# Two quantities in one PSUM bank per half of the heads, the u row spread by one product, and a new written-out order

## The chip, the cores and the metric

The kernel runs on one core of one Trainium2 chip. The metric is the device time of one launch in microseconds (us). The core has a tensor engine for matrix products (PE, with its weight loads shown as PEld), a vector engine (DVE), a scalar engine (ACT), a third elementwise engine (POOL), and a queue that does nothing here but issue DMAs (SP). Each engine takes its instructions strictly in the order in which the program lists them; between engines semaphores hold an instruction back until what it reads is there. Inputs and outputs lie in device memory and are moved by 16 DMA engines.

## The reference

```python
B, H, S, D = 4, 8, 768, 48                       # r, k, v, w: [B, H, S, D]; u: [H, D]
state = zeros(B, H, D, D)
for t in range(S):
    cur   = einsum('bhd,bhe->bhde', u * k_t, v_t)
    y_t   = einsum('bhd,bhde->bhe', r_t, state + cur)
    state = w_t[..., None] * state + einsum('bhd,bhe->bhde', k_t, v_t)
x = y.transpose(0, 2, 1, 3).reshape(3072, 384)
h = x @ w_in                                     # [384, 2048]
out = maximum(0.01 * h, h) @ w_out               # [2048, 384], float32 out
```

It is a recurrent attention with a decay w per channel, whose output goes through two dense layers with a leaky rectifier between them. The kernel computes the attention in chunks of time steps. Within a chunk the decays are summed as logarithms, r is multiplied by exp of the sum and k by exp of minus the sum; products of the two (scores), masked to earlier steps and multiplied by v, give the part of y from inside the chunk, and the state carried from the chunk before gives the rest. The u term is added through the sum over d of u, k and r, times v.

## The kernel before, in words

The 3072 rows are 24 chunks of 128 steps (n = 0 to 23), six for each of the four sequences. The first four chunks are handled as two **pairs** by `pair` (n = 0 and n = 2): 256 steps of one sequence at a time, two neighbouring steps (j = 0, 1) on one partition, so 128 partitions hold 256 steps. The other chunks go through `single`, alone or two together (`run`). The dense layers run over 14 blocks of one or two chunks (`BLOCKS`): steps `up` (first layer: six products of 128x256 for a block of two chunks, or twelve of 128x128 for a block of one), `g` (the rectifier on ACT, PSUM to SBUF), `down` (second layer: four products of 128x384 per step, four steps per chunk), `ocopy` (PSUM to SBUF) and `store` (a DMA on SP).

A pair runs through these steps: `ln` of w (ACT); `cum`, products with fixed triangular matrices that sum the logarithms (PE); `total`, the sum over a chunk, and `adep`, its exp; four exps (ACT, in PSUM); four `rk` products of exp with r or k (DVE, the tiles `rk`); PE transposes of `rk` into PSUM, copied to the tile `rkT` by ACT or DVE; `scores` (PE), masks (DVE, tile `m`), then `intra`, `inter` and the u term's `addvs` (PE), a copy to `y`, transposes of y and copies into `xT`, the input of `up`. Beside it POOL makes `ru` (u times k, times r) and `vs`, DVE sums it (`dg`), and POOL casts v to bf16 (`vb`). Pair 0 does this in two halves of the heads (`PARTS`), each of its exps, `rk` products and copies being half as wide (128x192); pair 2 does it with all heads at once (128x384). In each case one PSUM bank holds one of four quantities: exp for k at j = 0 and 1, exp for r at j = 0 and 1.

The row u (384 numbers) is loaded by a DMA on ACT's queue, split by DVE into bf16 parts, and spread over 128 partitions by three PE products with one row each (`u_spread`), then copied to `ub`. Before that the PE multiplies zeros (`zero`).

A single chunk has `ln`, `cum`, `ci`, two exps (`er`, `ek`), two `rk`, transposes by PE or, for the chunks of `RK_DMA`, by a DMA transpose on SP (rkT<-rk), `scores`, two masks, `sums` and `state`, `intra`, `yadd`, and transposes of y by PE or, for `Y_DMA`, by DMA (xT<-y).

The order of all steps, and the engine of each, is not made at run time: `TABLE` lists them in one sequence (P is PE, V DVE, A ACT, G POOL, S SP, Z a product of zeros), `HOMES` says which buffer of a pool each step's tile takes, and `Steps.issue` writes them out. A buffer that is to be reused makes the later step wait for its readers. Lines: `mult`'s tensor operations are L231, `copy`'s L237 (DVE) and L239 (ACT), all PE products but the transposes L242, transposes L353 and L384, the pair's loads L400, its `ln` L417, its exps L456, weights' loads L299, single chunks' loads L618, `g` L858, stores L830.

Of the kernel before, what the change touches and what calls it, by code (L numbers as in the profile page):

```python
# [8 lines left out]
BF16 = mybir.dt.bfloat16  # L9
AF = mybir.ActivationFunctionType  # L10
# [53 lines left out]
PARTS = {0: [(0, 2), (2, 4)]}  # L64
HALVES = 'wkr'
# [6 lines left out]
WIDE = {'rkT', 'm', 'y', 'rk'}  # L72
TABLE = """
A0 S11 P1066 S6 A1 S9 S7 S8 V2 S10 V3 S12 Z512 Z512 Z512 Z512 Z512 Z512 Z256 Z192 P4 S88 A13 Z128 P16 V5 P17 A27
P15 A26 S153 A14 A24 Z512 Z160 P18 V31 G58 A25 P19 V28 A40 P21 S89 A43 V37 G62 P32 A41 V44 P29 A22 V53 P1067 P38
A33 P45 V30 A23 P54 V34 A39 P20 G59 S90 V46 P35 V55 A42 V50 A36 V47 P51 G63 P70 V60 A52 P48 A92 V71 G61 S147 V64
P94 V72 G57 S145 P93 A102 P95 G65 V49 A99 P96 S91 P73 A101 G56 P81 A98 V75 A97 P76 A100 G154 P77 V74 P79 S151
V106 P66 S156 G121 P78 V103 P107 A82 V67 P104 G117 P83 V108 A105 P80 P68 V112 A84 V85 G155 P113 A69 V109 A114
P86 V148 A87 P110 G118 S149 A111 P740 S159 A146 G122 P129 V119 P132 V131 A741 P732 S162 G116 V134 P730 G120 A733
V123 P738 G115 A731 V130 G124 A152 P125 V133 P136 A739 V126 S165 P138 P135 S171 P137 P127 A158 V157 P736 S168  # L80
V139 A128 P742 S173 V142 A737 P140 V150 P744 A743 A141 P143 P734 A745 V144 P758 V161 G160 A735 P768 A759 P760
A769 P752 A761 V163 P746 A164 S252 P770 P762 A771 P766 V167 A763 G166 S201 P764 A175 A767 P177 P772 S172 A765
V178 P753 A179 S200 A773 P754 A180 V169 G170 P747 S231 V181 P748 A256 P183 S174 P749 V184 G216 P258 S202 V750
P755 A260 A261 V259 P774 G187 A756 S253 V182 A263 P775 A262 G188 P185 A204 S757 P780 V186 S229 V189 P206 P191
S203 V207 P776 V193 A208 G176 P777 S295 A209 V192 G190 P194 P781 A778 V211 G217 A195 V210 P196 P214 S254 P782
V197 A215 G270 V265 P198 P212 V218 S232 A199 P783 A213 P268 A233 P790 S230 V269 A784 P220 A791 G205 P235 S785
V222 P788 G219 A238 A237 S356 V236 P223 P786 A789 G297 S327 V221 G251 A224 P792 A787 V264 S292 G274 P225 A239
P266 A793 P794 V226 G234 A240 V241 P227 G271 P795 V267 S779 A228 V242 P243 S255 P804 G247 V272 A244 S324 P245
A805 P278 G248 P802 V246 S293 V279 P275 A803 G358 V249 P796 G329 V284 G250 P797 S294 V276 A296 P806 V285 A798
S353 P298 V277 A807 P800 G257 V299 S799 P280 G273 A801 P286 S326 P288 V281 A303 P808 S376 V287 A328 A302 V289  # L90
P282 P330 G310 A300 P809 V305 S355 A283 A332 V331 A301 P290 P308 G311 A291 P810 V304 A335 V309 S436 P822 G314
A334 V312 A333 P306 A357 P824 G313 S325 A823 P359 A307 G343 V336 P318 P826 S378 A362 V319 A361 A825 G375 P315
V360 A380 P811 S354 V317 A364 P382 A827 V316 P828 S377 A385 A812 V383 P820 A829 G449 P320 S419 A386 P814 A821
V321 G339 A363 P816 V337 S416 A815 V365 P347 A387 G340 P322 V388 P818 S338 A817 V348 A384 P390 A819 P367 G398
V366 P830 A368 V391 S437 G371 V341 P402 P369 P831 V389 S473 A370 G342 V403 P392 P832 V323 A393 G372 P846 S751
A420 P399 G421 V373 A847 S435 G394 P422 V408 S418 P842 A425 A424 V401 G434 P344 A843 P833 S813 V423 G374 S417
V346 P848 A427 A834 G450 V400 P844 A849 S492 V409 P404 A426 G395 P850 A845 V451 S835 V405 P836 S471 V396 A439
P406 V345 P837 A407 S491 V428 P441 P349 A443 P838 V442 S633 V350 A444 P851 A445 G453 V429 A446 P351 V447 P839
G430 S438 V352 P458 V448 P858 A840 V459 G431 S454 P862 A859 P860 A475 V432 A863 P477 G433 P856 A861 V478 S841
G504 P864 A479 S490 A857 P866 A482 G646 A865 P872 A867 G505 P870 A480 A481 S545 P873 G440 A871 V506 S379 G489  # L100
P874 V483 P466 G452 P455 S524 V467 P852 V457 S472 P853 V465 P868 A494 V464 S543 A854 P496 V456 A869 P468 P878
V497 S474 V469 A499 P460 A501 G381 P879 S470 A500 V461 G397 A498 P410 V503 P412 A528 V411 P462 P880 S544 A463
V413 G508 P530 V484 S581 P414 P875 A533 V502 G485 A415 S493 V531 P881 A876 G486 A535 P888 V882 S877 A532 A534
P884 G476 S509 V487 A889 G542 P898 A885 P513 A547 G488 P916 V514 A899 P549 G557 A917 S883 P890 V550 S526 P894
G558 A552 A553 P912 A891 V555 G495 A895 V559 P896 G507 A551 A554 P519 S525 P886 A913 G561 V556 S598 A897 P892
V520 A887 P510 S546 A893 P900 V512 P920 S599 V517 P914 V518 S601 P901 V536 A915 V511 G538 P521 S579 P902 V537
G539 V522 A602 P515 S562 P903 V516 G560 P604 V540 A904 P918 V605 G548 P906 A607 G612 A919 S523 P574 A608 P907
V575 A609 G603 P908 A606 V611 G616 P909 A583 P627 P585 V910 P921 S905 A588 V628 A587 S580 G597 P922 V586 S600
# [881 lines left out]
```

## Time and profile before

| | us |
|---|---|
| median of 3 runs | 182.56 (180.97 to 182.56) |
| the profiled execution | 181.88 |
| its span in the profile | 180.1 |
| PE busy in the span | 171.3 |
| ACT busy | 118.6 |
| DVE busy | 112.2 |
| POOL busy | 101.3 |

A span runs from the first to the last instruction; the time of an execution holds 1.8 us more. A row of the timeline gives start, duration, engine, line, operation, what it writes and reads, and how many instructions were merged; in brackets, how long the engine had been idle and what ended that. A row of a group gives the total busy time and the mean of one instruction in ns. A busy PE is not a PE at its peak, since its products overlap; how long one takes in a stream is read from the start of a row and the start of the next.

### The profile page before, as it was taken

The page shows a single profiled execution, that of the slowest core. Times are in us where ns is not written, and L with a number is a line of the kernel's source. Part 1 is how long each engine was busy: PE and PEld are TensorE (multiplying, and loading weights), DVE is VectorE, ACT ScalarE, POOL GpSimd, SP SyncE. Part 2 cuts the span into 40 slices and gives each one's busy share as a digit, 9 for nine tenths or more (in the row PEclk, how much of TensorE's full clock was granted, in tenths as well). Part 3 has the DMA queues.
Part 4 walks back from the last instruction along what each step waited for, and adds up shares of the span by engine and source line. Part 5 has one row for each costly group of instructions (what it writes and reads, how often), then busy time and mean ns, then how long its engine had stood idle before and what let it go on. Part 6 is the DMA issues. An engine that isn't in the chain of part 4 may idle for free.

```text
span 180.1 us, 5012 instructions
## 1 busy us (share of the span) xinstructions
PE 171.3 (95%) x1960; PEld 128.1 (71%) x1960; DVE 112.2 (62%) x230; ACT 118.6 (66%) x265; POOL 101.3 (56%) x137
## 2 busy tenths in 40 slices
PE   7978899999999999999999999989999999999992
PEld 2645688766878787778777977577786786876860
DVE  7489882459688879796398587686396384070000
ACT  3676987855966898667757954555776953722821
POOL 6799722467695858947946928567068378000000
PEclk9999999999999999999999999999999999999999
DMA  5999999799998989989999999999899998403202
GB/s 147 265 315 297 346 375 333 177 202 221 177 224 159 227 156 204 231 197 195 206 186 146 244 192 165 197 218 223 201 185 169 191 216 103 126 2 91 87 0 87
DMA packets 117129, 34.60 MB, mean 192 GB/s; under 512 B 109681, under 2 KB 116338, under 8 KB 117106
## 3 DMA queue, kind: packets, MB, share of 16 engines
q1 hardware_dynamic: 117104, 34.28, 91.6%
q8 instruction: 15, 0.25, 0.6%
q14 instruction: 8, 0.07, 0.2%
q10 hardware_dynamic: 2, 0.00, 0.0%
HBM read 25.17 MB, written 4.72 MB: 166 GB/s over the span
## 4 chain that ended last, share of the span: by engine, by line
PE 61%; DMA 12%; ACT 7%; POOL 6%; DVE 5%; issue 5%; SPq 2%; POOLq 0%; DVEq 0%; ACTq 0%
PE ps L242 59%; DMA in<-in_w_dram 6%; DMA in<-in_r_dram 3%; POOL ru L231 3%; DMA xT<-y 2%; DVE rk L231 2%; DVE m L231 2%; ACT g L858 2%; PE ps L353 1%; SPq L618 1%; ACT ps L651 1%; POOL sb L231 1%; POOL vs L231 1%; ACT lw L626 1%; POOL vb L235 1%
## 5 line engine op out<-in xcount | busy, mean ns | idle before, releaser
L242 PE MATMUL ps<-xT,w_in_b 128*128 128x256 bf16 (+1 forms) x672 | 70.6, 257 | 0.9 <-DMA xT<-y 0.6
L242 PE MATMUL ps<-w_out_b,g 128*128 128x384 bf16 x384 | 71.4, 326 | 0.0
L858 ACT ACTIVATE g<-ps 128x512 bf16<-128x512 f32 x96 | 56.4, 597 | 14.5 <-PE ps L242 12.3
L242 PEld LDWEIGHTS <-w_in_b 128*128 128x128 bf16 x672 | 57.1, 98 | 8.8 <-issue 0.8
L242 PEld LDWEIGHTS <-g 128*128 128x128 bf16 x384 | 34.7, 97 | 18.9
L231 DVE TENSOR_TENSOR m<-ps,maskb 128x512 bf16<-128x512 f32 x40 | 25.3, 683 | 9.9 <-PE ps L242 9.6
L231 DVE TENSOR_TENSOR rk<-ps,in 128x384 bf16<-128x384 f32 (+1 forms) x52 | 26.2, 520 | 7.9 <-ACT ps L651 2.6
L231 POOL TENSOR_TENSOR ru<-in,ub 128x384 f32<-128x384 f32 x24 | 23.8, 1001 | 11.5 <-DMA in<-in_k_dram 11.2
L231 POOL TENSOR_TENSOR sb<-s,a 128x384 bf16<-128x384 f32 x18 | 14.9, 830 | 17.3 <-ACT a L647 13.9
L231 POOL TENSOR_TENSOR ru<-ru,in 128x384 f32<-128x384 f32 x24 | 23.8, 1001 | 0.8
L239 ACT COPY o<-ps 128x384 f32<-128x384 f32 x19 | 9.1, 480 | 16.1 <-PE ps L242 16.0
L231 POOL TENSOR_TENSOR vs<-in,dg 128x384 f32<-128x384 f32 x20 | 16.5, 830 | 1.6 <-DVE dg L367 1.6
L235 POOL CAST vb<-in 128x384 bf16<-128x384 f32 x24 | 12.0, 504 | 8.4 <-DMA in<-in_v_dram 8.4
L367 DVE TENSOR_REDUCE dg<-ru 128x8 f32<-128x384 f32 x24 | 13.1, 547 | 5.3 <-POOL ru L231 5.1
L231 DVE TENSOR_TENSOR ci<-ps,lw 128x384 f32<-128x384 f32 x20 | 11.1, 555 | 6.6 <-PE ps L242 3.6
L231 DVE TENSOR_TENSOR y<-ps,vs 128x384 bf16<-128x384 f32 x20 | 11.1, 553 | 4.2 <-PE ps L242 4.2
L242 PEld LDWEIGHTS <-rkT 48*128 48x128 bf16 (+2 forms) x304 | 10.6, 97 | 3.5 <-issue 1.7
L626 ACT ACTIVATE lw<-in 128x384 bf16<-128x384 f32 x20 | 10.3, 521 | 3.1 <-DMA in<-in_w_dram 3.1
L647 ACT ACTIVATE a<-ps 64x4 f32<-64x4 f32 x36 | 6.1, 169 | 8.3 <-PE ps L242 4.2
L651 ACT ACTIVATE ps<-ps 128x384 f32<-128x384 f32 x20 | 9.6, 481 | 2.3 <-DVE ci L231 2.0
L654 ACT ACTIVATE ps<-ci 128x384 f32<-128x384 f32 x20 | 9.8, 496 | 0.9 <-DVE ci L231 0.9
L353 PE MATMUL ps<-ident,rk 128*128 128x128 bf16 x88 | 9.0, 227 | 1.4 <-DVE rk L231 1.2
(75 smaller groups left out, 164.3 us busy)
## 6 DMA issues: line engine op xcount, KB each, us to landing
out_dram<-o SPq DMA_DIRECT2D x24, 192.0 KB, 3.4
in<-in_r_dram SPq DMA_DIRECT2D x22, 192.0 KB, 4.3
in<-in_w_dram SPq DMA_DIRECT2D x22, 192.0 KB, 4.1
in<-in_k_dram SPq DMA_DIRECT2D x22, 192.0 KB, 4.3
in<-in_v_dram SPq DMA_DIRECT2D x20, 192.0 KB, 4.3
in<-in_moe_w_out_dram SPq DMA_DIRECT2D x4, 768.0 KB, 10.4
in<-in_moe_w_in_dram SPq DMA_DIRECT2D x2, 768.0 KB, 7.0
in<-in_moe_w_in_dram SPq DMA_DIRECT2D x4, 384.0 KB, 7.5
```

Source lines behind the costliest of these rows:

```text
L231: (nc.gpsimd if e == "POOL" else nc.vector).tensor_tensor(out=o, in0=a, in1=b, op=op)
L235: nc.gpsimd.tensor_copy(out=o, in_=i)
L239: nc.scalar.copy(out=o, in_=i)
L242: nc.tensor.matmul(o, lhsT=a, rhs=b, start=start, stop=stop, skip_group_check=True)
L353: nc.tensor.transpose(view()[:, g - g0, :], rk.t[:, kind, 2 * g : 2 * g + 2, :].rearrange("p h d -> p (h d)"), ident[:])
L367: "dg", "DVE", lambda e: nc.vector.tensor_reduce(out=dg.t[:], in_=ru.t[:], axis=AX.X, op=ALU.add),
L618: lambda e, src=src, i=i: nc.sync.dma_start(out=part(i)(), in_=src[b, :, t0 : t0 + L, :].rearrange("h p d -> p h d")),
L626: "ln", "ACT", lambda e: nc.scalar.activation(out=lw.t[:, :, 0:D], in_=wv(), func=AF.Ln),
L647: lambda e, q0=q0: nc.scalar.activation(out=a_in.t[q0 : q0 + 64, :, q0 // 64], in_=cp.t[q0 : q0 + 64, DM : DM + NP], func=AF.Exp),
L651: "er", "ACT", lambda e: nc.scalar.activation(out=heads(cp.t), in_=heads(cp.t), func=AF.Exp),
L654: "ek", "ACT", lambda e: nc.scalar.activation(out=heads(ek.t), in_=ci.t[:], func=AF.Exp, scale=-1.0),
L858: lambda e, hp=hp, g=g, j=j, J=J, N=N: nc.scalar.activation(out=g.t[:, j : j + J, 0:N], in_=hp.t[:, 0 : J * N].rearrange("p (a n) -> p a n ...
```

## The change

- **Pairs.** Both pairs are now split into two halves of the heads. In each half, one PSUM bank holds both j of k's exponent and another both j of r's, side by side (2 x 192 columns). So a half has two exps, two `rk` products and two copies of transposes, each on 384 columns (the copies on 512), where pair 0 had four of half that width in each half; pair 2 had four of 384 columns for all heads and still has four. Each bank is made by four `cum` products of 192 columns. Scores and masks of pair 2 go by halves of the heads, not by j. Pair 2's w is loaded in two halves (`HALVES`).
- **u.** DVE places the three parts of u in rows 0, 32 and 64 of a zeroed tile, and one PE product with all 128 rows replaces the three with one row.
- **v.** The cast of v may go to ACT as well as to POOL.
- **Order.** `TABLE` and `HOMES` are new throughout. Of the casts of v ten go to ACT; POOL has one cast of weights in place of five; DVE has eleven output copies in place of five and seven copies into `xT` in place of three. Pair 0's loads are issued in the order w, w, k, k, r, r (halves) instead of r, w, k, w, k, r; the weights' loads come after all loads of pair 2 instead of among them. No store stands ahead of the last load of a chunk, where seventeen did before; all 24 are issued behind it: six ahead of the last DMA transpose of `rk` (n = 22, 23), three more ahead of the last but one DMA transpose of y (n = 20, 21), ten more ahead of the last one (n = 22, 23), and five after it. The zero products before the first `cum` are seven of 512 columns and two of 256, without a pause.

```diff
-PARTS = {0: [(0, 2), (2, 4)]}
-HALVES = 'wkr'
+HALVES = {0: 'wkr', 2: 'w'}
...
-    def u_spread(e):
-        for x, t in enumerate([u_row, *u_parts]):
-            mm(u_ps.t[:, 0:DM], ones_f[:], top(t.t), x == 0, x == 2)
-    s_u = step("u_mm", "PE", u_spread, deps=[chain[-1]], reads=[u_row, *u_parts], takes=[u_ps])
+    def u_rows(p):
+        return u_top.t[p : p + 1, :, :].rearrange("p h d -> p (h d)")
+
+    s_z = step("u_zero", "DVE POOL", lambda e: (nc.gpsimd if e == "POOL" else nc.vector).memset(u_top.t[:], 0.0),
+               at=-3, takes=[u_top])
+    s_u0 = step("u_split", "DVE", lambda e: copy(e, u_rows(0), top(u_row.t)), deps=[u_raw, s_z], reads=[u_row], takes=[u_top])
+    s_u1 = step("u_split", "DVE", lambda e: mult(e, u_rest.t[0:1, :], u_row.t[0:1, :], top(u_row.t), ALU.subtract),
+                deps=[u_raw], reads=[u_row], takes=[u_rest])
+    s_u2 = step("u_split", "DVE", lambda e: copy(e, u_rows(32), top(u_rest.t)), deps=[s_u1, s_z], reads=[u_rest], takes=[u_top])
+    s_u3 = step("u_split", "DVE", lambda e: mult(e, u_rows(64), u_rest.t[0:1, :], top(u_rest.t), ALU.subtract),
+                deps=[s_u1, s_z], reads=[u_rest], takes=[u_top])
+    s_u = step("u_mm", "PE",
+               lambda e: mm(u_ps.t[:, 0:DM], ones_b[:], u_top.t[:].rearrange("p h d -> p (h d)"), True, True),
+               deps=[s_u0, s_u2, s_u3], reads=[u_top], takes=[u_ps])
...
-        return vb, step("vb", "POOL", lambda e: copy(e, vb.t[:], vv()), at, deps=vl, reads=slots, takes=[vb])
+        return vb, step("vb", "POOL ACT", lambda e: copy(e, vb.t[:], vv()), at, deps=vl, reads=slots, takes=[vb])
...
-        parts = PARTS.get(n, [(0, NP)])
+        parts = [(0, NP // 2), (NP // 2, NP)]
...
-        def cum(x, bank, mats):
-            g0, g1 = parts[x]
+        def cum(x, bank, both, j2, mats):
+            h0, h1 = 2 * parts[x][0], 2 * parts[x][1]

             def go(e):
-                for j in range(2):
-                    mm(heads(bank.t)[:, 2 * g0 : 2 * g1, :], mats[j][:], lw.t[:, j, 2 * g0 : 2 * g1, 0:D], j == 0, j == 1)
+                for q in range(2):
+                    mm(quantities(bank.t)[:, q], both[:], lw.t[:, j2, h0:h1, 0:D], q == 0, False)
+                for q in range(2):
+                    mm(quantities(bank.t)[:, q], mats[q][:], lw.t[:, 1 - j2, h0:h1, 0:D], False, True)
...
-            c1, c0, cg, e0 = (Bf("ps", "cp2") for _ in range(4))
-            banks.append([c1, c0, cg, e0, cum(x, c1, (tstr2, tinc2)), cum(x, c0, (tinc2, tinc2)), cum(x, cg, (tstr2, tstr2))])
+            kb, rb = Bf("ps", "cp2"), Bf("ps", "cp2")
+            banks.append((kb, rb, cum(x, kb, tstr2, 0, (tinc2, tstr2)), cum(x, rb, tinc2, 1, (tinc2, tstr2))))
...
-            s_k0 = exp(x, c1, e0, -1.0, [s_c1], [e0])
-            s_r1 = exp(x, c1, c1, 1.0, [s_c1, s_k0], [])
-            s_k1 = exp(x, cg_, cg_, -1.0, [s_cg], [])
-            s_r0 = exp(x, c0, c0, 1.0, [s_c0], [])
...
+            for a, bank, s_c, scale in ((1, kb, s_kb, -1.0), (0, rb, s_rb, 1.0)):
                 name, si, off = ("r", 1, 0) if a == 0 else ("k", 0, 1)
+                s_e = step(
+                    "exp2", "ACT",
+                    lambda e, bank=bank, scale=scale: nc.scalar.activation(
+                        out=bank.t[:, 0 : 2 * HW], in_=bank.t[:, 0 : 2 * HW], func=AF.Exp, scale=scale),
+                    n, deps=[s_c], reads=[bank])
                 s_d = step(
-                    "rk2" + half, "DVE",
-                    lambda e, a=a, j=j, bank=bank, si=si, off=off, h0=2 * g0, h1=2 * g1: mult(
-                        e, rk[j].t[:, a, h0:h1, 0:D], heads(bank.t)[:, h0:h1, :], view(si, off, j)()[:, h0:h1, :]),
+                    "rk2", "DVE",
+                    lambda e, a=a, bank=bank, si=si, off=off, h0=2 * g0, h1=2 * g1: mult(
+                        e, rkw.t[:, :, a, h0:h1, 0:D], quantities(bank.t),
+                        slots[si].t[:, off * 768 : (off + 1) * 768].rearrange(
+                            "p (h j d) -> p j h d", h=H, j=2)[:, :, h0:h1, :]),
...
+                tr = Bf("ps", "tr")
...
+                def tpose(e, tiles=tiles, a=a, g0=g0, g1=g1):
+                    for j in range(2):
+                        for g in range(g0, g1):
+                            nc.tensor.transpose(
+                                tiles()[:, j, g - g0, :], rkw.t[:, j, a, 2 * g : 2 * g + 2, :].rearrange("p h d -> p (h d)"),
+                                ident[:])
...
+                s_tr = step("tr", "PE", tpose, n, deps=[s_d], reads=[rkw], takes=[tr])
+                s_T[x].append(step("tr_copy", "DVE ACT", tcopy, n, deps=[s_tr], reads=[tr], takes=[rkTb]))
```

More of the change, by code (lines that the diff above doesn't have):

```diff
@@ L414, in pair @@
         lw = Bf("lw2")
+        HW = DM // 2
         s_lns = [step(
-            "ln2" + half, "ACT",
+            "ln2_h", "ACT",
             lambda e, h0=2 * g0, h1=2 * g1: nc.scalar.activation(
@@ L450, in pair @@
             n, deps=[s_tot], reads=[cg], takes=[a_in]) for q0 in (0, 64)]
[L452 to L462 removed]
+        rkw, rkTb = Bf("rk", wide=2), Bf("rkT", wide=2)
         def rkT():
```

173 lines of the change are left out of this document (79 added, 94 removed).

## The prediction

> **What bounds the kernel now.** I read the page first, then stretches of the span, then the front in order of time.
>
> ```profile
> PE 171.3 (95%) x1960; PEld 128.1 (71%) x1960; DVE 112.2 (62%) x230; ACT 118.6 (66%) x265; POOL 101.3 (56%) x137
> ...
> DMA  5999999799998989989999999999899998403202
> ...
> q1 hardware_dynamic: 117104, 34.28, 91.6%
> ```
> ```profile
> 25.00:36.00 11.00, 10.88 (x94) 8.69 (x92) 4.89 (x10) 9.45 (x18) 3.17 (x3) 1.00 0.96 278
> 45.90:82.70 36.80, 36.37 (x509) 29.11 (x507) 30.29 (x61) 28.63 (x70) 27.82 (x35) 1.00 1.02 198
> 120.00:150.00 30.00, 30.00 (x331) 23.19 (x329) 18.45 (x35) 21.12 (x47) 17.94 (x23) 1.00 1.07 196
> ```
>
> PE is busy 95% of the span. In the stretches (length; then busy us of PE, weight loads, DVE, ACT, POOL) it leaves 0.12, 0.43 and 0.00 us idle. So from about 25 us on the end is set by how much PE still has to do, and a change can win only what PE loses before that, the few waits after it, and the tail. The DMA engines are nearly as full until about 150 us (slice digits 8 and 9, queue share 91.6%), so transfers can become the bound by being late. The front:
>
> ```profile
> 0.81 0.45 SPq L400 DMA_DIRECT2D in<-in_r_dram  x1
> 1.26 3.12 PE L242 MATMUL ps<-zeros 128*128 128x512 bf16 x8 [1.26 <-DVE zeros L246]
> 1.32 0.49 SPq L400 DMA_DIRECT2D in<-in_w_dram  x1
> ...
> 4.25 0.53 ACT L417 ACTIVATE lw<-in 128x384 bf16<-128x384 f32 x1 [1.62 <-DMA in<-in_w_dram]
> 4.30 1.14 PE L242 MATMUL ps<-o,ones_f 1*128 1x384 bf16 x3
> 5.45 0.53 PE L242 MATMUL ps<-lw,tinc 128*128 128x192 bf16 x2
> 7.36 1.59 DVE L231 TENSOR_TENSOR rk<-ps,in 128x192 bf16<-128x192 f32 x5 [1.33 <-ACT ps L456]
> 7.43 1.96 POOL L231 TENSOR_TENSOR ru<-in,ub 128x384 f32<-128x384 f32 x2 [1.04 <-DMA in<-in_k_dram]
> 9.27 0.33 PE L242 MATMUL ps<-lw,tstr 128*128 128x192 bf16 x2
> 13.64 1.29 DVE L231 TENSOR_TENSOR m<-ps,mask 128x512 bf16<-128x512 f32 x2 [0.72 <-PE ps L242]
> 18.84 0.81 PE L242 MATMUL ps<-xT,w_in_b 128*128 128x256 bf16 x6 [0.24 <-ACT xT L239]
> 21.79 1.28 DVE L231 TENSOR_TENSOR m<-ps,mask 128x512 bf16<-128x512 f32 x2
> 22.70 0.52 PE L242 MATMUL ps<-vb,rk 64*128 64x96 bf16 x16 [0.40 <-POOL vb L235]
> 24.30 1.47 PE L242 MATMUL ps<-xT,w_in_b 128*128 128x256 bf16 x12
> ```
>
> Pair 0's masks end at 13.64 + 1.29 = 14.93, the first dense group starts at 18.84, pair 2's masks end at 21.79 + 1.28 = 23.07. The last idle of PE in the front is the 0.40 us before 22.70.
>
> **The change part by part.** Prices per instruction:
>
> ```profile
> L231 DVE TENSOR_TENSOR rk<-ps,in 128x384 bf16<-128x384 f32 x44 | 23.7, 551 | 6.5 <-ACT ps L651 2.6 <-ACT ps L654 2.3 <-ACT lw L626 0.7
> L367 DVE TENSOR_REDUCE dg<-ru 128x8 f32<-128x384 f32 x24 | 13.1, 547 | 5.3 <-POOL ru L231 5.1
> L235 POOL CAST vb<-in 128x384 bf16<-128x384 f32 x24 | 12.0, 504 | 8.4 <-DMA in<-in_v_dram 8.4
> L231 DVE TENSOR_TENSOR m<-ps,mask 128x512 bf16<-128x512 f32 x8 | 5.2, 685 | 1.1 <-PE ps L242 1.1
> L237 DVE COPY rkT<-ps 128x512 bf16<-128x512 bf16 x8 | 3.4, 420 | 3.1 <-PE ps L353 3.1
> L237 DVE COPY o<-ps 128x384 f32<-128x384 f32 x5 | 2.8, 556 | 5.4 <-PE ps L242 5.4
> L237 DVE CAST w_in_b<-in 128x768 bf16<-128x768 f32 x3 | 2.6, 863 | 0.4 <-DMA in<-in_moe_w_in_dram 0.4
> L231 DVE TENSOR_TENSOR rk<-ps,in 128x192 bf16<-128x192 f32 x8 | 2.5, 350 | 1.4 <-ACT ps L456 1.3
> L456 ACT ACTIVATE ps<-ps 128x192 f32<-128x192 f32 x8 | 2.3, 313 | 1.4 <-PE ps L242 1.2
> L456 ACT ACTIVATE ps<-ps 128x384 f32<-128x384 f32 x4 | 1.8, 475 | 0.7 <-PE ps L242 0.6
> L237 DVE CAST y<-ps 128x384 bf16<-128x384 f32 x3 | 1.6, 545 | 0.0
> L231 DVE TENSOR_TENSOR sb<-ps,a 128x384 bf16<-128x384 f32 x2 | 1.1, 553 | 0.2 <-PE ps L242 0.2
> L231 DVE TENSOR_TENSOR o<-o 1x384 f32<-1x384 f32 x2 | 1.1, 544 | 0.0
> L237 DVE COPY xT<-ps 128x384 bf16<-128x384 bf16 x3 | 1.1, 352 | 0.2 <-PE ps L384 0.2
> ```
>
> *Wider operations.* Pair 0: eight `rk` at 0.350 become four at 0.551, 2.80 to 2.20 us on DVE; eight exps at 0.313 become four at 0.475, 2.50 to 1.90 on ACT. Pair 2 had four of 0.551 and four of 0.475 already and keeps them. So 0.6 us goes on each engine, in pair 0 alone. The new `rk` writes two strided blocks, which no row shows: from 0.551 up to twice the half form, 0.70; I take 0.551, the row of the same element count, and keep 8 x 0.15 = 1.2 us for the range.
>
> *Loads in front.* A first transfer before is r (0.81), the second w (1.32), landed at 4.25, when `ln` starts; the fifth, half of k, released POOL at 7.43. That is (7.43 - 4.25) / 3 = 1.06 a half. In the new order w is first, so `ln` can start about 0.5 sooner (0.81 against 1.32), but r's halves are fifth and sixth: 7.4 and 8.5. The new DVE order begins with r of half 2. So the first `rk` starts at about 7.45, not sooner than before (7.36): the earlier `ln` and the 0.6 us of exps are hidden behind r.
>
> *u.* One product replaces three, 1.14 us (4.30) less some 0.4; four row operations on DVE (at most 0.544 each, 2.2) replace two. DVE waits for its first exp until 7.36 anyway, and the u parts would be done by about 6. Nothing. If that cover were gone, `ub` and POOL's `ru` would be 1.1 us late; `vs` is needed only by `addvs`.
>
> *Pair 0 on DVE*, in the new order: four `rk` (2.20), a copy (0.42), two `dg` (1.09), four masks (2.74), `sb` (0.55), 7.0 us without a gap: 7.45 + 7.0 = 14.5, against 14.93. *Pair 2*: four `rk`, y, two copies, `sb`, two `dg`, four masks: 2.20 + 0.55 + 0.84 + 0.55 + 1.09 + 2.74 = 8.0, so masks end at 22.4, against 23.07. Each gap adds to it, and there is no cover: 0 to 1.0, since the present order spends 23.07 - 14.93 = 8.1 on a like list, with one cast more.
>
> *What PE has done by then.* Before, at 22.70, four dense groups (a group of six is 0.65: 24.30, (1.47 - 0.27) / 11 x 6) are issued and 24.30 - 22.70 = 1.6 us of pair 2 remain: 4 x 0.65 - 1.6 = 1.0. After, the order puts two groups ahead of the last masks and all of pair 2 with them (both leave y's transposes): 1.3 at 22.5. That is 0.5 ahead (0.3 of work, 0.2 of time). But the next groups need two weight casts that stand on DVE behind the last mask, 0.863 + 0.545 (y) + 0.863: the fifth group at 22.4 + 2.3 = 24.7, while PE runs out at about 24.3, after 0.1 lost before. That returns 0.5. **Front: 0.**
>
> *Cum.* Six products of 384 and twelve of 192 columns become 32 of 192, 1536 columns more: 0.6 us at the price below (0.162 per 384), all within the front, where PE waits for DVE: nothing.
>
> ```profile
> 50.17 0.40 PE L353 MATMUL ps<-ident,rk 128*128 128x128 bf16 x4 [0.34 <-DVE rk L231]
> 117.67 1.59 PE L242 MATMUL ps<-xT,w_in_b 128*128 128x256 bf16 x13 [0.59 <-DMA xT<-y]
> 171.20 5.36 PE L242 MATMUL ps<-w_out_b,g 128*128 128x384 bf16 x32
> out_dram<-o SPq DMA_DIRECT2D x24, 192.0 KB, 3.4
> xT<-y SPq DMA_TRANSPOSE x6, 3.5
> ```
>
> *Stores behind the loads.* 91.6% of 180.1 is 165 us for 34.28 MB; by bytes a store of 0.197 MB is 0.95 us of all engines. Seventeen leave the stretch before the last load: up to 16 us of room in a nearly full queue. PE's idle there is 0.34 (an `rk` that waited) and 0.59 (a DMA transpose), 0.9 in all; I take half: **-0.5**, bounds -0.9 and 0.
>
> *DVE load.* Six output copies (3.3), four copies into `xT` (1.4), a cast of w_out and the u rows come to DVE. From the first group of block 2 to that of block 6 (45.9 to 82.7) the listed instructions at their rows' prices sum to 34.4 on DVE before and 36.2 after, with PE's work alike (37.0, 36.7). DVE is busy 30.3 of 36.8 there; 5% more is 31.9, 87%. Bounds 0 and +1.8; **+0.2**. POOL loses ten casts (5.0) and four of weights; nobody on the end's path waits for that.
>
> *Tail.* The last DMA transpose of y is issued behind ten stores that the order spreads over some 5.5 us of PE's work. From that `yadd` to the first group of the last block PE has six groups and two steps of four 384 products, 6 x 0.65 + 2 x 0.65 = 5.2; `yadd` 0.55 and the median landing 3.5 leave 1.1. The three stores right ahead cost 0 (they fit) to 2.85: bounds 0 and +1.7; **+0.3**, since the order spaces them. The last two stores are now 0.65 apart on the queue, nothing.
>
> **Sum.** 0 - 0.5 + 0.2 + 0.3 = 0. On the profiled execution (181.88: span 180.1 and 1.8 around it) that is 181.9, 0.7 under the median of the runs shown (182.56).
>
> **Rivals.**
>
> *The front's gain is kept* (faster). The casts are not late (-0.5), the DMA waits go (-0.9), DVE's and the tail's extra cost nothing, and DVE's starts overlap (five `rk` of 0.350 took 1.59, not 1.75), 15.0 us of it 5% shorter (-0.7): 181.9 - 0.5 - 0.4 - 0.5 - 0.7 = 179.8. For it: no engine is over 66%. Against: r lands late. The PE itself may help: two products of 192 columns took 0.53 us at 5.45 and 0.33 at 9.27, so PE ran at half rate until past 5.45. [...]
>
> *DVE in order is the bound* (slower). Each copy of transposes, mask and `yadd` that DVE does late stalls PE in order. Place: 7.4 to 22.4, where it has no gap, and 45 to 83. Price: 1.0 of gaps, 0.6 for wider `rk` in the front, 1.6 more in the stretch: 185.1 at most, 184.0 typically. It decides once DVE's share passes about 95%. For: the sums of durations are 36.2 against PE's 36.7. Against: 87% by the busy count.
>
> *Stores hold up the last transposes* (slower): 181.9 - 0.3 + 1.7 = 183.3, or 184.2 with the same at the transposes of `rk`. [...]
>
> *The change does not do what it says*: "half as many" holds for pair 0 only; that is in the forecast.
>
> **How the numbers follow.** Forecast 0.43; gain kept 0.27; DVE 0.21; stores 0.09. One per cent, 1.8 us, is about what a measurement can tell here. Faster takes the first rival; slower takes DVE, and most of the stores: 0.29; same: 0.44. Range: 179.6 at the first rival, 184.6 within the second.
>
> **What would show it.** First `rk` at 7.4 to 7.5 behind r's load; pair 0's masks ending near 14.5, pair 2's near 22.4; PE idle some 0.5 before 24.7; DVE near 32 of 37 us from block 2 to 6; PE's rows without gaps over 0.3 to the last block, and there a wait on xT<-y under 0.5. The prediction is wrong if DVE's front has gaps of over 1 us, or if PE waits repeatedly on DVE between 40 and 90 us.

## The result

The changed kernel takes 180.66 us, the median of ten executions (179.61 to 182.13), against 182.29 of the kernel before beside it (ten, 180.97 to 183.25). The ratio is 0.9913, with a 95% interval of 0.9886 to 0.9941. Ratios here and below leave out executions more than 1.5% above the fastest of their kernel, so they need not be the quotient of the medians. The change is within one per cent; the time is in the forecast's range of 179.6 to 184.6, and 1.2 below its 181.9. The profiled execution took 180.65, its span 178.8, against 181.88 and 180.1.

### The profile page after: what moved, and what is told of

The parts are those of the page before. It is cut to its first block, busy times and chain, and to the rows that moved or that the text cites. A ratio compares the mean times of both kernels' runs of the same rounds, so it can differ in the third digit from the quotient of the medians.

```text
span 178.8 us, 5037 instructions
## 1 busy us (share of the span) xinstructions
PE 170.6 (95%) x1970; PEld 128.6 (72%) x1970; DVE 116.2 (65%) x238; ACT 119.1 (67%) x263; POOL 93.1 (52%) x123
## 4 chain that ended last, share of the span: by engine, by line
PE 82%; DMA 6%; SPq 4%; DVE 3%; ACT 2%; issue 1%; POOL 0%; DVEq 0%
PE ps L240 79%; SPq L631 3%; DMA in<-in_v_dram 3%; DMA in<-in_r_dram 3%; DVE rk L229 1%; SPq L398 1%; PE ps L351 1%; PE ps L382 1%; ACT rkT L237 1%; ACT vb L237 0%; ACT w_in_b L237 0%; DVE rkT L235 0%; DVE y L229 0%; DVE y L235 0%; POOL vb L233 0%
## 5 line engine op out<-in xcount | busy, mean ns | idle before, releaser
L240 PE MATMUL ps<-w_out_b,g 128*128 128x384 bf16 x384 | 70.4, 326 | 0.0
L871 ACT ACTIVATE g<-ps 128x512 bf16<-128x512 f32 x96 | 55.9, 598 | 20.0 <-PE ps L240 17.6
L240 PEld LDWEIGHTS <-w_in_b 128*128 128x128 bf16 x672 | 56.4, 98 | 7.3 <-ACT w_in_b L237 0.4
L240 PEld LDWEIGHTS <-g 128*128 128x128 bf16 x384 | 35.5, 98 | 19.5
L229 DVE TENSOR_TENSOR rk<-ps,in 128x384 bf16<-128x384 f32 x48 | 25.4, 552 | 6.3 <-ACT ps L667 3.2
L237 ACT COPY o<-ps 128x384 f32<-128x384 f32 x13 | 6.2, 477 | 12.1 <-PE ps L240 11.9
L229 DVE TENSOR_TENSOR y<-ps,vs 128x384 bf16<-128x384 f32 x20 | 10.8, 553 | 4.4 <-PE ps L240 1.5
L233 POOL CAST vb<-in 128x384 bf16<-128x384 f32 x14 | 7.0, 503 | 5.7 <-DMA in<-in_v_dram 5.7
L229 DVE TENSOR_TENSOR s<-ps,sb 128x384 f32<-128x384 f32 x14 | 7.7, 552 | 3.1 <-PE ps L240 3.1
```

What stands on the lines that cost most here:

```text
L229: (nc.gpsimd if e == "POOL" else nc.vector).tensor_tensor(out=o, in0=a, in1=b, op=op)
L233: nc.gpsimd.tensor_copy(out=o, in_=i)
L237: nc.scalar.copy(out=o, in_=i)
L240: nc.tensor.matmul(o, lhsT=a, rhs=b, start=start, stop=stop, skip_group_check=True)
L871: lambda e, hp=hp, g=g, j=j, J=J, N=N: nc.scalar.activation(out=g.t[:, j : j + J, 0:N], in_=hp.t[:, 0 : J * N].rearrange("p (a n) -> p a n ...
```

## The profile after

First the page of the changed kernel: busy time by engine, the load of the DMA engines in 40 slices, the share of the DMA queue, then the groups and DMA issues that answer to those of before (busy us and mean ns of one; KB and median us to landing).

```profile
PE 170.6 (95%) x1970; PEld 128.6 (72%) x1970; DVE 116.2 (65%) x238; ACT 119.1 (67%) x263; POOL 93.1 (52%) x123
...
DMA  5999999899998989999999999999799995820022
...
q1 hardware_dynamic: 117120, 34.29, 92.7%
...
L229 DVE TENSOR_TENSOR rk<-ps,in 128x384 bf16<-128x384 f32 x48 | 25.4, 552 | 6.3 <-ACT ps L667 3.2
...
out_dram<-o SPq DMA_DIRECT2D x24, 192.0 KB, 2.2
```

PE is as full as before, and DVE has the 4 us more that the moved copies brought. The wide `rk` costs 552 ns like the others. A store lands in a median of 2.2 us, not 3.4. (That median says little: it is 2.2 in `stores_back` below too, with 16 stores among the loads, where 3.4 was expected.) The front, DVE in order of time:

```profile
7.54 1.95 DVE L229 TENSOR_TENSOR rk<-ps,in 128x384 bf16<-128x384 f32 x4 [0.84 <-DMA in<-in_r_dram]
...
12.71 1.28 DVE L229 TENSOR_TENSOR m<-ps,mask 128x512 bf16<-128x512 f32 x2
14.13 0.56 DVE L229 TENSOR_TENSOR rk<-ps,in 128x384 bf16<-128x384 f32 x1
...
20.71 1.29 DVE L229 TENSOR_TENSOR m<-ps,mask 128x512 bf16<-128x512 f32 x2 [0.38 <-PE ps L240]
21.92 0.68 DVE L235 CAST w_in_b<-in 128x768 bf16<-128x768 f32 x1
22.52 0.54 DVE L235 CAST y<-ps 128x384 bf16<-128x384 f32 x1
22.98 0.94 DVE L235 CAST w_in_b<-in 128x768 bf16<-128x768 f32 x1
```

Pair 0's masks end at 12.71 + 1.28 = 13.99 (14.93 before), pair 2's at 22.00 (23.07 before), and the second cast of weights at 23.92. PE at that place:

```profile
22.29 1.48 PE L240 MATMUL ps<-xT,w_in_b 128*128 128x256 bf16 x12
23.61 0.50 PE L382 MATMUL ps<-ident,y 128*128 128x128 bf16 x6
23.98 6.29 PE L240 MATMUL ps<-xT,w_in_b 128*128 128x256 bf16 x56
```

No bracket stands behind these rows: the view lists no idle time of PE here. At 23.98 it has four dense groups, all of pair 2 and y's transposes behind it. Before, at 24.30, it had four groups and pair 2, with y's transposes (2 x 0.17) still to do. So the front is 0.32 of time and 0.34 of work, 0.66 us, ahead, in these two executions. From 25 us to the end PE has one wait that is worth a row, where it had two (0.34 and 0.59). The last row below is the tail, where PE runs the last `down` steps without a pause:

```profile
56.96 0.33 PE L240 MATMUL ps<-vb,rk 128*128 128x96 bf16 x4 [0.89 <-POOL vb L233]
...
164.37 10.56 PE L240 MATMUL ps<-w_out_b,g 128*128 128x384 bf16 x64
```

The stretch from the first group of block 2 to that of block 6, and the one before the tail (length; busy us of PE, weight loads, DVE, ACT, POOL; clock, DMA share, GB/s):

```profile
45.56:81.78 36.22, 35.33 (x513) 28.82 (x512) 32.31 (x67) 27.59 (x67) 29.32 (x36) 1.00 1.08 180
120.00:150.00 30.00, 30.00 (x333) 22.66 (x331) 20.08 (x39) 18.80 (x43) 14.16 (x17) 1.00 0.94 203
```

The 0.89 idle of PE in the first stretch is the one wait above. DVE is busy 32.3 of 36.2 and holds nobody up.

## Experiments

The theory after the result: 0.7 to 0.8 us come from the front, because the casts of weights are not late, and some 0.5 from transfers that wait less, because the stores are gone from among the loads. Rivals: PE reaches its full rate sooner through the u product; the width of the instructions is the whole front; the stores are the whole gain. Ratios below are to the kernel before beside the run, with the 95% interval.

**The changed kernel again**, as the measure.

> The changed kernel once more, without any edit, as the measure for the kernels beside it on the same chip: 180.3 to 181.0.

Measured: 179.73 us, 0.9887 (0.9836 to 0.9937), a little below what was expected. Its profile has a span of 177.3, and PE waits nowhere behind 25 us (rows of PE in the front, then one of the windows):

```profile
23.03 0.50 PE L382 MATMUL ps<-ident,y 128*128 128x128 bf16 x6
23.40 2.79 PE L240 MATMUL ps<-xT,w_in_b 128*128 128x256 bf16 x24
```
```profile
45.00:70.00 25.00, 25.00 (x352) 20.69 (x350) 22.75 (x48) 21.55 (x53) 22.18 (x28) 1.00 1.10 181
```

So the wait at 56 us comes and goes from one execution to the next, and the front's lead over the kernel before is 1.24 here (23.40 in place of 23.98), 0.66 there. The 0.58 between the two and the wait of 0.89 make up the 1.5 us between the spans. The front is ahead of the first profile from its first `rk` on, since r landed sooner, and there the load of k for pair 2 is the next to be waited for:

```profile
7.02 1.95 DVE L229 TENSOR_TENSOR rk<-ps,in 128x384 bf16<-128x384 f32 x4 [0.47 <-DMA in<-in_r_dram]
...
13.77 0.56 DVE L229 TENSOR_TENSOR rk<-ps,in 128x384 bf16<-128x384 f32 x1 [0.29 <-DMA in<-in_k_dram]
```

Pair 0's masks end at 13.48 in this profile. So one and the same program moves by 0.5 us in the front with the landing of one load, and a single profile of a variant can't tell less than that.

**Stores back among the loads.** The stores in `TABLE` move back to some 24 entries behind their copies; 16 of them then stand ahead of the last load.

```diff
 # TABLE, the store of chunk 0 (its copy is A740), with its neighbours
-S867 V683 P982 A682 S741 V970 S901
+V197 S220 P181 A198 S741 P767 A199
```

> The changed kernel with each store of the output issued soon behind its copy, 17 of them among the loads as before, instead of behind the last load. Theory (stores among the loads make transfers late): two or three waits of PE on transfers of 0.3 to 0.6 appear between 45 and 120 us, a store lands in a median of 3.4 again in place of 2.2, and the time is 181.0 to 181.6. Rival (the moved stores brought nothing, the loads are early enough either way): 180.5 to 180.8.

Measured: 185.74 us, 1.0154 (1.0100 to 1.0207): far more than either expected. Between 45 and 150 us PE waits eight times; these are the five longest, in order of time:

```profile
57.59 0.32 PE L240 MATMUL ps<-lw,trev 128*128 128x384 bf16 x1 [0.51 <-ACT lw L639]
...
83.23 0.34 PE L382 MATMUL ps<-ident,y 128*128 128x128 bf16 x3 [0.54 <-DVE y L229]
...
100.83 0.82 PE L240 MATMUL ps<-xT,w_in_b 128*128 128x256 bf16 x6 [0.35 <-ACT xT L237]
...
110.92 0.32 PE L240 MATMUL ps<-lw,trev 128*128 128x384 bf16 x1 [0.96 <-ACT lw L639]
...
133.73 0.83 PE L240 MATMUL ps<-xT,w_in_b 128*128 128x256 bf16 x6 [0.32 <-DMA xT<-y]
```

All eight add up to 3.3 us. Not all of this profile's lag is theirs: at the fifth dense group it is already 1.9 us behind the first profile of the changed kernel (25.84 against 23.98), ahead of any store: in this execution the granted clock of PE was 0.50 from 10.8 to 17.6 us (last section). Against that profile the lag grows by 4.0 us between 50 and 150 us, and that is the part of the stores. Four of the six executions, at a mean clock of 1.0, take 183.93 to 186.74, so the medians' distance does not hang on the clock. The last two loads are issued from 144.70 on there and from 133.21 on in the second profile of the changed kernel, 2.4 of that being the front (the queue's rows, `stores_back` above, the changed kernel below):

```profile
144.70 1.14 SPq L631 DMA_DIRECT2D in<-in_v_dram  x2
```
```profile
133.21 1.71 SPq L631 DMA_DIRECT2D in<-in_v_dram  x2
```

**The same places, small stores**, to tell bytes from places on the queue. The kernel leaves out 124 of the 128 rows of these 16 output chunks.

```diff
-        step("store", "SP", lambda e: nc.sync.dma_start(out=rows[ch], in_=o.t[:]), ch, deps=deps, reads=[o])
+        n = 4 if ch in SMALL else L
+        step("store", "SP", lambda e: nc.sync.dma_start(out=rows[ch][0:n], in_=o.t[0:n, :]), ch, deps=deps, reads=[o])
```

> The changed kernel with the stores put back behind their copies, as in the earlier run at 185.7, but the 16 of them that stand ahead of the last load write only 4 of their 128 rows (the rest of these output chunks is left out); places, waits and order on the queue stay. Theory (a store costs by its bytes: 0.197 MB, some 0.95 us of all DMA engines, which the loads behind it are late by): the waits of PE between 45 and 150 us, 3.3 us in eight places in that run, go but for one or two of under 0.4, the last load is issued near 134 us instead of 145, and the time is 179.3 to 180.8. Rival (it is the places on the queue: each store waits for its copy and holds the loads behind it): most of the waits stay, 183 to 185.5.

Measured: 179.88 us, 0.9882 (0.9836 to 0.9929). One wait is left, the known one, and the last two loads are issued from 136.07 on:

```profile
56.72 0.33 PE L241 MATMUL ps<-vb,rk 128*128 128x96 bf16 x4 [0.80 <-POOL vb L234]
```

So what `stores_back` lost is not due to the places nor to the waits on the queue; it goes with what the stores move (here the rows, and with them the bytes, are 4 of 128).

**The kernel before with its stores late.** The other corner of the square.

```diff
 # TABLE of before, the first of 17 stores (S684 is the last load), with its neighbours
-A262 G188 P185 A204 S757 P780 V186 S229
+P988 V676 A974 G649 S757 P674 V677 S975
```

> The kernel before with one edit: its 17 stores among the loads are issued behind the last load, some of them among the last transposes, as the change does; all else as it was. Theory A (the stores' move is a gain by itself, of the two waits on transfers that PE has, 0.9 us at most): 181.2 to 181.8 against 182.0 to 182.3. Theory B (the move is worth 4 to 5 us wherever it is made, as putting the stores back cost the changed kernel; the rest of the change loses 3): 177.5 to 178.5. Theory C (the move is worth much only together with the change's order of loads, which leaves less time between a landing and its use): 181.0 to 182.3, and no wait on a transfer of over 0.3 us is left from 45 to 150 us or the few that are left are not on transfers.

Measured: 181.07 us, 0.9964 (0.9932 to 0.9995). That is nearest to theory A, a little below its 181.2 to 181.8, and its two waits are gone (windows, columns as above):

```profile
45.00:70.00 25.00, 24.95 (x355) 20.38 (x354) 20.37 (x41) 21.45 (x53) 17.98 (x24) 1.00 1.05 172
70.00:95.00 25.00, 25.00 (x310) 19.18 (x308) 18.83 (x38) 17.21 (x41) 18.19 (x22) 1.00 0.97 166
95.00:120.00 25.00, 25.00 (x301) 19.45 (x299) 18.74 (x36) 16.25 (x40) 16.27 (x21) 1.00 0.87 162
```

In this execution the same products run 1.39 us faster than in the profile before from 43 to 118 us, more than the 0.93 of the two waits; the rest lies in pauses too short to be listed. Its span is only 0.6 shorter because it had lost 0.77 by 43 us, with a mean granted clock of 0.80 in the first 25 us (1.00 in the profile before).

The four corners are: order of before, stores early 1 and late 0.9964; new order, stores early 1.0154 and late 0.9887 to 0.9913. The new order loses 1.5% with the stores early, and with them late it wins 0.5 to 0.8% over the old order with late stores. Theory C as a statement on the pair of changes holds too: the move is worth 0.4% in the one order and some 2.5% in the other.

**u by three products of one row** (the rest of u's row work unchanged; the three rows lie in a corner of `w_out_b` that is not yet in use).

```diff
-        return u_top.t[p : p + 1, :, :].rearrange("p h d -> p (h d)")
+        return w_out_b[0:1, p // 32, :]
...
-               lambda e: mm(u_ps.t[:, 0:DM], ones_b[:], u_top.t[:].rearrange("p h d -> p (h d)"), True, True),
+               lambda e: [mm(u_ps.t[:, 0:DM], ones_b[0:1, :], u_rows(p), p == 0, p == 64) for p in (0, 32, 64)],
```

> The changed kernel with u spread as before, by three products of one row each; its row operations on DVE stay, and only put their results into one row. Theory (the front's gain comes from half as many exps and products on DVE, and the first rk waits for r's load): the first rk stays at 7.5 us, pair 0's masks end within 0.2 of 13.99, and the time is 180.7 to 180.9 against 180.66 of the changed kernel. Rival (the one product of 128 rows brings PE to its full rate early, by 6.8 us of the span against past 7.2 before, and that is the gain): the products of cum behind it run at half rate until about 9 us, the front is 0.5 or more later, 181.3 to 181.8.

Measured: 180.09 us, 0.9851 (0.9806 to 0.9897). The time is below both expectations. The first `rk` starts at 7.16, behind its exp, not at 7.5, and pair 0's masks end at 13.65, between the changed kernel's 13.48 and 13.99. The one wide product brings nothing that shows; the rival on PE's rate falls. The row that would have shown it:

```profile
5.42 0.72 PE L240 MATMUL ps<-w_out_b,ones_b 1*128 1x384 bf16 x3
6.08 0.42 PE L240 MATMUL ps<-lw,tinc 128*128 128x192 bf16 x3
```

Three products of 192 columns behind the one-row products take 0.42, against 0.68 at a granted clock of 0.50 (`narrow`, 16.27), so PE is at its full rate there without the wide product. In the changed kernel's first profile three such products right behind the wide one take 0.69 (5.90), in its second 0.41 (5.79): when the full rate begins differs between executions of one program.

**Pair 0's exps and `rk` at half width.**

```diff
-                    lambda e, bank=bank, scale=scale: nc.scalar.activation(
-                        out=bank.t[:, 0 : 2 * HW], in_=bank.t[:, 0 : 2 * HW], func=AF.Exp, scale=scale),
+                    lambda e, bank=bank, scale=scale: [nc.scalar.activation(
+                        out=bank.t[:, lo:hi], in_=bank.t[:, lo:hi], func=AF.Exp, scale=scale)
+                        for lo, hi in ([(0, HW), (HW, 2 * HW)] if n == 0 else [(0, 2 * HW)])],
 # and rk2 in the same way, one mult for each quantity
```

> The changed kernel with the exps and rk products of pair 0 each in two instructions of half the width, one for each quantity, on the same banks. Theory (width is the front's gain): eight rk at about 0.32 in place of four at 0.49 hold DVE 0.6 to 0.8 longer; pair 0's masks end at 14.6 to 14.8, pair 2's at 22.5, PE has an idle of about 0.5 before 25 us, and the time is 181.2 to 181.4. Rival (the front's length is set by the loads and by PE, not by DVE's list): the masks end later by the same, but the dense groups make up for it, 180.7 to 180.9.

Measured: 181.05 us, 0.9915 (0.9879 to 0.9951), not to be told from the changed kernel. Eight narrow `rk` hold DVE 2.21 us, four wide ones 1.95, so width saves 0.26 there and not 0.6. On ACT eight narrow exps take 2.46 in two rows (0.66 and 1.80), four wide ones 1.89 in the second profile of the changed kernel (0.47 and 1.42): there it is 0.57. The first `rk`:

```profile
7.55 2.21 DVE L229 TENSOR_TENSOR rk<-ps,in 128x192 bf16<-128x192 f32 x8 [1.01 <-ACT ps L468]
```

It starts behind its exp. The first mask starts at 10.76, against 10.60 and 10.08 in the two profiles of the changed kernel. What comes later in this profile can't be compared, since PE's granted clock fell from 1.00 to 0.50 at 11.3. By time the rival "width is the whole front" falls: the six executions at a mean clock of 0.995 or more have a median of 180.31, as the eight such of the changed kernel's first run have 180.39.

**r third among the loads** (w, w, r, k, r, k), then **r fourth** (w, w, k, r, k, r) **with the bonus sums behind masks.**

```diff
 # r_early
-A0 S9 P1056 S10 A1 S11 S12 V2 S14 V4 S13 V3
+A0 S9 P1056 S10 A1 S14 S12 V2 S13 V4 S11 V3
 # front2
-A0 S9 P1056 S10 A1 S11 S12 V2 S14 V4 S13 V3
+A0 S9 P1056 S10 A1 S12 S14 V2 S11 V4 S13 V3
...
-V45 P58 A28 A42 G46 P55 V60 A41 S137 V49 A78 P64 P51 V56 A79 S141 G50
+P58 A28 P55 V60 V45 A42 G46 A41 S137 A78 P64 P51 V56 V49 A79 S141 G50
```

> The changed kernel with pair 0's loads in the order w, w, r, k, r, k (halves of the heads) in place of w, w, k, k, r, r. Theory (r's landing holds the first rk at 7.54): the first rk starts at 6.8 to 7.0 behind its exp; the last half to land is now one of k, wanted by the last rk, so that one starts at 8.6 to 9.0 and pair 0's masks end 0.3 to 0.6 sooner; the time is 180.1 to 180.4. Rival (POOL's products with k set the bonus, and they start up to 1 us later): addvs late, 180.7 to 181.5.

> The changed kernel with pair 0's loads in the order w, w, k, r, k, r, and with its two sums over the bonus on DVE each one place later, behind a mask. Theory (r's landing holds the first rk, and in the try with r third it was POOL's products with k, through the sums over them, that held the masks): the first rk starts at 6.7 to 6.9 behind its exp, the masks of pair 0 end 0.2 to 0.6 sooner than 13.99, and the time is 179.4 to 180.1. Rival (POOL, whose products start with the last half of k at 7.1 to 7.4, holds the bonus and with it y of pair 0): y later by 0.3 to 0.6, 180.2 to 181.0.

Measured: 183.63 us, 1.0062 (1.0027 to 1.0096), and 180.96 us, 0.9920 (0.9886 to 0.9954). In both the first `rk` starts at 6.82 behind its exp, so r's landing did hold it. With r third, POOL's products with k come late and the sums over them hold DVE, and with it the masks:

```profile
6.82 1.95 DVE L229 TENSOR_TENSOR rk<-ps,in 128x384 bf16<-128x384 f32 x4 [0.28 <-ACT ps L468]
...
11.01 0.55 DVE L365 TENSOR_REDUCE dg<-ru 128x8 f32<-128x384 f32 x1 [1.47 <-POOL ru L229]
```

With that mended, pair 0's masks end at 13.66, sooner than in the changed kernel's first profile (13.99) but not than in its second (13.48), and pair 2 waits for its own load of k:

```profile
12.38 1.28 DVE L229 TENSOR_TENSOR m<-ps,mask 128x512 bf16<-128x512 f32 x2
13.91 0.56 DVE L229 TENSOR_TENSOR rk<-ps,in 128x384 bf16<-128x384 f32 x1 [0.25 <-DMA in<-in_k_dram]
```

So that load is the next late thing at pair 0's end, as in the second profile of the changed kernel. I had not put it among the bounds. Further on, this profile of `front2` has a wait of PE of 1.37 at 64.42, behind an `rk`.

**The cast ahead of the fifth group made twice.**

```diff
-                    lambda e, x=x, y=y: copy(
-                        e, w_in_b[:, :, x * 256 : (x + 1) * 256], staged()[:, :, y * 256 : (y + 1) * 256]),
+                    lambda e, x=x, y=y: [copy(
+                        e, w_in_b[:, :, x * 256 : (x + 1) * 256], staged()[:, :, y * 256 : (y + 1) * 256])
+                        for _ in range(2 if x == 2 else 1)],
```

> The changed kernel with the cast of the third piece of w_in on DVE (0.94 us, it ends at 23.92 in the changed kernel's trace, and the fifth dense group, which needs it, starts at 23.98) made twice in a row. Theory (that cast ends just in time, by less than 0.1; the forecast had it 0.4 late): an idle of PE of 0.7 to 0.9 appears ahead of the fifth group, and the time is 0.7 to 0.9 above the changed kernel, 180.7 to 181.2. Rival (PE has other slack there, or a later wait swallows it): within 0.3 of the changed kernel.

Measured: 180.72 us, 0.9922 (0.9883 to 0.9960). The wait appears at once, in the size expected (the cast, then PE):

```profile
22.54 1.93 DVE L235 CAST w_in_b<-in 128x768 bf16<-128x768 f32 x2
...
24.53 1.70 PE L240 MATMUL ps<-xT,w_in_b 128*128 128x256 bf16 x14 [0.86 <-DVE w_in_b L235]
```

Its profile's span is 178.3, 1.0 above the 177.3 of the changed kernel's profile that also waits nowhere behind the front. Between the medians the difference is smaller than their intervals, so the rival is not excluded by time. In the profiles the cast ends just ahead of its use, as the rows 23.92 and 23.98 say.

**Output copies on ACT; one load of v earlier.**

```diff
 # copies_on_act: eleven output copies
-V746 V774 V824 V844 V872 V900 V914 V936 V970 V964 V992
+A746 A774 A824 A844 A872 A900 A914 A936 A970 A964 A992
 # v6_early
 # TABLE, SP's steps alone
-S245 S316 S282 S222 S314
+S222 S245 S316 S282 S314
```

> The changed kernel with its eleven output copies that stand on DVE put on ACT, where all others are (before, five stood on DVE). Theory (DVE's in-order list is not what holds PE from 25 us on, nor is ACT's): 180.4 to 181.0, no new wait. Rival 1 (DVE's list holds PE in small steps): 0.5 or more faster, 179.4 to 180.1. Rival 2 (ACT, 119 of 178.8 us busy, takes over 5 us more and its activations of the dense products come late): 181.2 to 182.5, with waits of PE on g.

> The changed kernel with the load of v for the sixth single chunk issued four places earlier on the queue, ahead of three loads of w and v for later chunks. Theory (the one wait of PE over 0.5 us behind 25 us, 0.9 on vb at 56 us, is that load): the wait goes, and nothing takes its place, 179.6 to 180.1. Rival (the queue is full, and another load takes its place as the late one): 180.4 to 181.0, with a wait of 0.5 to 1 on another load's cast or logarithm between 50 and 70 us.

Measured: 180.76 us, 0.9935 (0.9898 to 0.9971), and 180.30 us, 0.9914 (0.9884 to 0.9943). Less work on DVE wins nothing. In the one profile with v sooner, waits on a cast of v and on a logarithm stand there instead:

```profile
53.50 0.33 PE L240 MATMUL ps<-vb,rk 128*128 128x96 bf16 x4 [0.65 <-ACT vb L237]
...
56.55 0.32 PE L240 MATMUL ps<-lw,trev 128*128 128x384 bf16 x1 [0.72 <-ACT lw L639]
```

That the move of v caused them is not shown. With nothing moved there, the place and size of this wait differ too: none in `again`, `cast_twice` and `copies_on_act`, 0.46 at 56.32 in `u_rows`, 0.96 at 56.71 in `filled`.

**Zeros where PE waits in the front.**

```diff
+                    if n == 0 and (a, g0) == (0, NP // 2):
+                        mm(tr.t[:], zeros[:, 0:128], zeros[:], True, True)
 # and one product of zeros ahead of each of pair 0's scores and of its first product with masks
```

> The changed kernel with four products of zeros (128x512 each) put where PE waits in the front: ahead of pair 0's first transposes, ahead of each of its two groups of scores, and ahead of its first product with masks. Theory (in some executions the granted clock of PE halves for some 7 us from about 11 us on, since PE does too little between 8 and 11 us; that is what spreads the times of all these kernels): with the zeros the mean granted clock is 0.995 or more in all executions or all but one, and no time is over 181.2; the median is 179.8 to 180.4. Rival (the halving has another cause): a mean clock of 0.98 to 0.99 in two or more executions, as in 3 of 16 of the changed kernel, and the zeros delay the chain by up to 0.4, 180.3 to 181.0.

Measured: 180.54 us, 0.9902 (0.9863 to 0.9940), eight executions of 179.48 to 181.82, all at a mean granted clock of 0.996 or more. The clock did as the theory expected, but two times lie above the 181.2 that it allowed, and the median is in the rival's range. So the clock is not all that spreads the times. What the run was for is told at the end.

None of these beats the changed kernel by more than the intervals allow.

## Why the prediction was right, and where it was not

*What bounds the kernel.* Right. PE sets the end from 25 us on; the gain came from what PE has done by 25 us and from what it loses after that.

*First `rk` behind r's load at 7.45.* Right in its cause, and in its number in one execution: 7.54, but 7.02 in the second profile. And the argument that r's landing hides the rest was short by one: behind it stands the load of pair 2's k (`front2`).

*Pair 0's masks at 14.5, pair 2's at 22.4.* They ended at 13.99 and 22.00. The lists were right, their sums too long, since I added durations where starts overlap: four wide `rk` took 1.95, not 2.20. The rival "the front's gain is kept" had that term, and the forecast should have had it.

*Front: 0.* **This is the step that failed.** It took 0.5 of lead and gave 0.5 back through two casts behind the last mask, ready at 24.7 while PE ran out at 24.3. They were ready at 23.92: 0.4 from the masks, and 0.4 from durations (0.863 + 0.545 + 0.863 = 2.3 forecast behind the masks; 22.00 to 23.92, 1.9, measured). PE asked for the second at 23.98. So nothing was given back, and the front is 0.66 ahead in the first profile and 1.24 in the second. `cast_twice` shows that there is no slack: with 0.99 more on that cast, 0.86 of idle time appears in front of the fifth group. Which part of the new front made the lead, no run isolates; taking back the wide product of u or the width of pair 0's instructions cost nothing that shows in the time.

*Wider instructions save 0.6 on each engine.* On ACT it is 0.57, on DVE 0.26 (`narrow`), for the same reason: eight narrow `rk` took 2.21 where the sum said 2.80. In the end's time it can't be told from nothing.

*u, nothing.* Right (`u_rows`).

*Stores behind the loads: -0.5.* Right for what it was worked out from: moved in the kernel before, they give 0.36% (0.66 us of 182, with an interval from 0.1 to 1.2), and both of its waits go. In the profiled execution one wait of 0.89 stands in the place of 0.93, in the other none. What I missed is that the late stores carry the new order: with them back it is 1.5% slower than the kernel before.

*DVE's load: 32 of 37 us, +0.2.* The load is right (32.31 of 36.22), the cost is 0: no wait of PE on DVE above 0.3 us between 40 and 90 us, and `copies_on_act` wins nothing. The rival's 95% of DVE's time, at which it was to become the bound, was a guess of mine that no run tests: 32.31 of 36.22 is 89%.

*Tail: +0.3.* For the transposes it is 0. The last DMA transpose stands behind ten stores on the queue, and PE's rows have no gap:

```profile
148.72 5.07 SPq L843 DMA_DIRECT2D out_dram<-o  x10
154.83 1.22 SPq L796 DMA_TRANSPOSE xT<-y  x1
```

So no run shows the 1.7 us that the rival on the last transposes adds here; a DMA transpose of y lands in a median of 2.9, where 3.5 was taken. Something else is longer there: from PE's last product to the end of the span it is 3.87 us in both profiles of the changed kernel, 3.51 before and in `stores_back`. The forecast had nothing for it, and why is not shown.

*The sum.* When PE starts the fifth group it has the same products left in both kernels, but for the 0.34 of transposes. To the end of the last one the kernel before takes 152.26 us; without the 0.34 and its two waits (0.93) that is 150.99. The changed kernel takes 150.96, without its wait 150.07, and 150.00 in the second profile. So 0.9 to 1.0 us is won in pauses too short to be listed as waits. The late stores may be a part of it (0.46 of that kind in `before_stores_late`); what the rest is stays open. Between the two spans, 180.07 and 178.81, the terms are: front -0.66, listed waits -0.04, short pauses -0.92, behind the last product +0.36, together -1.26. The forecast had 0, -0.5 for the waits, and +0.5 for DVE and the tail. Neither of the last two shows in these profiles, and that they cancel is luck: the number stayed within one per cent, but a forecast of no gain met a gain of 0.6 to 1.1%. The rival "the front's gain is kept", 179.8, was nearer in mechanism than the forecast: its casts, its overlap and its unharmed transposes are what was seen. "DVE in order" and "stores hold up the last transposes" did not happen.

## What to carry to other kernels

Where one engine is full from some point to the end, count what it has done by that point, and take the list ahead of it by starts, not by sums of durations: an error of 0.4 in the list made a cast late on paper that was just in time. Price a move of transfers in the order in which it will run, too: taking the stores from among the loads was worth 0.4% in the old order and 2.5% in the new one. And when a wait on a load goes, look at once for the load behind it; here pair 2's k stood right behind pair 0's r. Look at a second profile of the same program before a variant is read: here one landing moved the front by 0.5 us, and a wait of 0.9 came and went.

## What the runs showed that I had not expected

In some executions the granted clock of PE halves once, in the middle of the front. The rows are windows of `stores_back`, whose first 25 us are the same program as the changed kernel's:

```profile
9.00:10.50 1.50, 1.11 (x38) 0.74 (x36) 1.47 (x4) 1.36 (x5) 1.50 (x3) 1.00 1.27 261
10.50:11.00 0.50, 0.15 (x12) 0.05 (x1) 0.50 (x2) 0.50 (x3) 0.50 (x2) 0.80 1.29 264
11.00:17.00 6.00, 5.94 (x79) 3.74 (x80) 3.38 (x7) 3.00 (x10) 5.20 (x8) 0.50 1.19 304
17.00:18.00 1.00, 1.00 (x13) 0.97 (x12) 0.97 (x3) 0.85 (x3) 0.74 (x1) 0.69 1.06 387
```

The clock is 0.50 from about 10.8 to 17.6, 6.8 us. A whole execution with one such stretch has a mean clock near 0.981 (6.8 us at 0.50, of 184.3): 0.981 in this profile and that of `narrow`, 0.978 in that of `r_early`. Between 8 and 11 us PE was busy 2.13 of 3.00 here, where the clock falls at 10.8, and 2.67 in `narrow`, where it falls at 11.3, while 2.20 in `u_rows` and 2.32 in the changed kernel's first profile brought no fall. So the busy share of PE alone does not tell when the clock falls, and what does is not shown. PE's first products, too, differ between executions. Here they are from `stores_back`, and then from the changed kernel's first profile, which is the same program at that place and had no halving:

```profile
4.32 0.41 PE L240 MATMUL ps<-lw,tinc 128*128 128x192 bf16 x3
```
```profile
4.64 0.69 PE L240 MATMUL ps<-lw,tinc 128*128 128x192 bf16 x3
```

In the three profiles of kernels with this front that have the halving (`stores_back`, `narrow`, `r_early`) these three products take 0.41, PE being at its full rate already; in the others 0.58 to 0.69, and there is none. The granted clock reads 1.00 there in both cases. In these profiles an early full rate goes with a later halving.

How often it came is less clear. A mean clock of 0.992 or less was seen in all 12 executions of `r_early`, in which PE waits 1.90 us for the masks at 10 to 12 us, in 6 of 12 of `narrow`, in 3 of 16 of the changed kernel (both runs of it), and in none of 8 of `filled`. But it was also seen in none of the 11 of `v6_early`, whose front is the changed kernel's, so the step from 3 of 16 to 0 of 8 may be chance. In `r_early` the halved clock may be part of its 1.0062; no run parts it from the late masks.

The kernel before has such executions too: 34 of the 87 executions of it beside these runs have a mean clock of 0.992 or less. The gain does not come from that. In `again` and beside it, the executions above that have medians of 179.62 (5) for the changed kernel and 181.44 (16) for the kernel before.
